# Merging the sign of float64 weights with one two-input VectorE instruction, and moving GpSimd's remainder behind the next item's addition

## The chip, the cores and the metric

The program runs on one core of a Trainium2 chip. Its engines are TensorE (PE, with its weight loads as PEld), VectorE (DVE), ScalarE (ACT), GpSimd (POOL) and SyncE (SP, which here only issues DMAs). Each engine works through its own instructions in order and waits on semaphores for the others. The metric is the device time of one execution in microseconds: the kernel before took a median of 1064.12 us in 3 runs (1062.75 to 1064.14).

## The reference, cut to what matters

Three parts follow one another: attention over 4 batches and 8 heads of 768 tokens with a mask of 8 global and 96 local positions; a routed layer of 8 experts in which each expert takes 384 of the 3072 tokens; and a dense layer with a leaky activation. The two weights of the dense layer come in double precision, and the device itself turns them into the form that it computes with.

```python
def _attn_ref(q, k, v, n_global, n_local):
    scores = scale * np.matmul(q, k.transpose(0, 1, 3, 2)) + bias      # masked
    a = np.exp(scores - np.max(scores, axis=-1, keepdims=True))
    a = a / (np.sum(a, axis=-1, keepdims=True) + 1e-09)
    return np.matmul(a, v)
...
def _moe_ref(x, w_gate, w1, w2):
    ...
    for e in range(E):
        mask = assigned == e
        out[mask] = np.maximum(x[mask] @ w1[e], 0.0) @ w2[e]
...
def _moe2_ref(x, w_in, w_out, alpha):        # w_in 512 x 2048, w_out 2048 x 512
    h = x @ w_in
    g = np.maximum(h, 0.0) + alpha * np.minimum(h, 0.0)
    return g @ w_out
```

## The kernel before

**The stages.** Attention comes first and ends near 185 us of the span; a search for the tokens of the first expert follows; from about 217 us on the experts run, one after another, each through its own layer and then through the dense one, and TensorE is nearly full there to the end. The change touches only what is woven into attention.

**Attention** (L91 to L329) works through 48 steps: 24 groups of 128 queries, each in two halves of four heads (`steps`, L284). In step n the code issues the scores of step n + 1 (L186: TensorE, then L192 on VectorE, which adds the bias and takes the minimum, then L195 on ScalarE, the exponential), the transposes of step n (L207, copied out of PSUM by L211 on VectorE and L209 on ScalarE), `divisor` (L234, a tiny GpSimd instruction named `a_se`), the combination of step n - 2 (L238, L252, L261, L271 and, in the odd steps, L274), and the values of step n - 1 (L226, L229). A batch's first group has scores 128 wide, the others 232.

**The conversion of doubles** (class `Doubles`, L31 to L88) is a generator that attention pulls twice in a step, before the scores and at the step's end, in four of every five steps (`turn`, L280). The fifth is called a free step below. It has 32 items of 128 x 512 doubles, taken by turns from `w_in` and `w_out`: an **in item** (the 1st, 3rd, ...) ends as a pair of tensors, a rounded `hi` and the remainder `lo`, both in `wi`; an **out item** (the 2nd, 4th, ...) ends in `wo` after one addition. The raw doubles lie in `f_raw` (`f64_raw` in the code), as two 32-bit words each, so one word's elements are 8 bytes apart; `f_t` (`f64_t`) takes the result. Both have three buffers.

An item takes one step. On the first pull (`begin`, L69) ScalarE makes the absolute value of the high words (L72), GpSimd clamps it (L73), ScalarE scales the low words (L74). On the second (`join`, L76) VectorE shifts and masks `f_t` (L79) and writes the sign bit into `f_raw`'s low word (L80, on 16-bit elements), and GpSimd adds the two (L82). `finish` (L84) belongs to the item before: on the first pull, behind the new item's L73, GpSimd rounds to `hi` (L87) and subtracts for `lo` (L88), for in items only. Two more raw loads are ahead on SP's queue (L67), each waiting until the addition that last read its buffer is done.

**The order** is that in which the code issues, engine by engine: nothing is rearranged afterwards. VectorE's L79 and L80 stand at the end of a step, and the four L192 for the next scores stand behind them.

Of the kernel before, what the change touches and what calls it, by code (L numbers as in the profile page):

```python
# [9 lines left out]
FT = mybir.dt.float32  # L10
# [4 lines left out]
U16 = mybir.dt.uint16  # L15
AF = mybir.ActivationFunctionType
OP = mybir.AluOpType
# [13 lines left out]
class Doubles:  # L31
# [7 lines left out]
    def jobs(self, items):  # L39
        queue, begun = [], None  # L40

        def fetch():
            if items:
                src, dst, hi, lo = items.pop(0)
                queue.append(dict(src=src, dst=dst, hi=hi, lo=lo))
                self.load(queue[-1])

        fetch()
        fetch()
        yield  # L50
        yield
        while True:
            done, begun = begun, queue.pop(0) if queue else None
            fetch()
            if begun:
                self.begin(begun)
            if done:
                self.finish(done)
            yield
            if begun:  # L60
                self.join(begun)
            self.idle = not (queue or begun)
            yield

# [10 lines left out]

    def join(self, job):  # L76
        nc, t = self.nc, job["t"]
        parts = job["raw"].bitcast(U16).rearrange("p a (b c) -> p a b c", c=2)
        nc.vector.tensor_scalar(t, t, 3, 0x7FFFFFF8, op0=OP.logical_shift_left, op1=OP.bitwise_and)  # L79
        nc.vector.tensor_scalar(parts[:, :, 0, 1], parts[:, :, 1, 1], 0x8000, None, op0=OP.bitwise_and)  # L80
        dst = t if job["dst"] is None else job["dst"].bitcast(I32)
        nc.gpsimd.tensor_tensor(dst, t, job["raw"][:, :, 0], op=OP.add)  # L82

    def finish(self, job):  # L84
        if job["hi"] is not None:
            v = job["t"].bitcast(FT)
            self.nc.gpsimd.tensor_scalar(job["hi"], v, 1.0, 1.0, op0=OP.mult, op1=OP.mult)  # L87
            self.nc.gpsimd.tensor_tensor(job["lo"], v, job["hi"], op=OP.subtract)  # L88


def attention(ctx, tc, q, k0, k, v, vw, w_gate, n_global, n_local, ident, x_dram, logits, side, router):  # L91
# [1148 lines left out]
```

## Time and profile before

| | |
|---|---|
| median of 3 runs | 1064.12 us |
| profiled execution | 1064.48 us, of which the span from the first to the last instruction is 1062.8 us |
| busy over the span | PE 97%, DVE 68%, ACT 36%, POOL 51% |
| L80, 32 instructions | 750 ns median, 1835 ns longest |
| L79, 32 instructions | 419 ns median, 1355 ns longest |
| L82, 32 instructions | 1280 to 1307 ns |
| L88, 16 instructions | 1270 to 1502 ns |

The busy shares are means over stages with different limits. The stretch that matters here is the one in which the 32 items run, from about 26 to 172 us. In a view in order of time a row gives the start, the duration, the engine, the line and the tiles; instructions of one engine that don't wait for each other overlap a little in the records, so the price of one is read from start to start.

### The profile page before, as it was taken

How to read it: one execution, taken by the hardware profiler on the slowest of the kernel's cores; microseconds unless marked ns; L12 is line 12 of the kernel's file. 1: busy time of each engine (PE TensorE's matmuls, PEld its weight loads, DVE VectorE, ACT ScalarE, POOL GpSimd, SP SyncE). 2: the span in 40 equal slices, each digit the busy share in tenths (PEclk: the TensorE clock that was granted, in tenths of full speed). 3: DMA queues.
4: the chain of work that ended last, by engine and by line, in shares of the span. 5: the costliest groups of instructions: out<-in, count | busy, mean ns of one | idle time of the engine just before them, and what ended most of it. 6: DMA issues, size and time to landing. Idle time of an engine off the chain costs nothing.

```text
span 1062.8 us, 19360 instructions
## 1 busy us (share of the span) xinstructions
PE 1027.4 (97%) x6475; PEld 904.7 (85%) x6475; DVE 725.7 (68%) x2189; ACT 386.4 (36%) x984; POOL 544.0 (51%) x825
## 2 busy tenths in 40 slices
PE   7999999699999999999999999999999999999997
PEld 5777767389889988898899889988998999999996
DVE  6999998787878778877887688689854313231321
ACT  6989988143224212321232123212321232123211
POOL 4777764175669325733473347344642464247223
PEclk9999999699999999999999999999999999999999
DMA  9899893241355244326432633443353345434131
GB/s 299 275 298 308 293 306 125 51 148 60 132 196 166 86 168 157 105 104 194 143 115 85 220 118 118 148 155 116 121 172 123 122 138 170 133 106 169 63 136 69
DMA packets 89046, 164.98 MB, mean 155 GB/s; under 512 B 9812, under 2 KB 43092, under 8 KB 88948
## 3 DMA queue, kind: packets, MB, share of 16 engines
q1 hardware_dynamic: 85108, 151.18, 42.7%
q0 software_dynamic: 3840, 12.59, 3.5%
q8 instruction: 51, 0.84, 0.3%
q14 instruction: 47, 0.39, 0.1%
HBM read 142.76 MB, written 20.97 MB: 154 GB/s over the span
## 4 chain that ended last, share of the span: by engine, by line
PE 79%; DVE 8%; POOL 4%; issue 3%; ACT 3%; DMA 2%; SPq 0%; POOLq 0%; ACTq 0%; DVEq 0%
PE m_h L969 23%; PE m_acc L1014 23%; PE m_acc L956 12%; PE m_h L929 12%; PE a_pt L207 2%; PE a_xp L226 2%; PE a_s L186 2%; ACT a_p L195 2%; DVE f_raw L80 1%; POOL m_so L898 1%; POOL m_g L898 1%; PE a_cb L252 1%; DVE a_sx L192 1%; PE m_h L855 1%; DMA f_raw<-in_moe_w_out_dram 1%
## 5 line engine op out<-in xcount | busy, mean ns | idle before, releaser
L898 POOL TENSOR_TENSOR m_g<-m_t,m_g 128x192 fp32r<-128x192 f32 (+1 forms) x286 | 163.8, 595 | 335.0 <-ACT m_g L978 334.9
L1014 PE MATMUL m_acc<-m_so,m_g 128*128 128x512 f32 x1143 | 294.1, 399 | 0.0
L969 PE MATMUL m_h<-m_y,wi 128*128 128x384 f32 x1536 | 290.2, 339 | 0.0
L969 PEld LDWEIGHTS m_h<-m_y,wi 128*128 128x128 f32 x1536 | 267.4, 188 | 6.6 <-DVE m_xt L871 0.2
L1014 PEld LDWEIGHTS m_acc<-m_so,m_g 128*128 128x128 f32 x1143 | 209.2, 189 | 34.5 <-POOL m_g L898 0.5
L898 POOL TENSOR_TENSOR m_s<-m_r,m_s 128x256 fp32r<-128x256 f32 x256 | 187.4, 756 | 77.7 <-ACT m_s L888 77.4
L978 ACT ACTIVATE m_g<-m_t 128x384 fp32r<-128x384 f32 (+1 forms) x143 | 70.0, 489 | 427.0 <-DVE m_t L977 251.3
L976 DVE TENSOR_SCALAR m_t<-m_h,m_al 128x384 f32<-128x384 f32 (+1 forms) x144 | 82.3, 571 | 155.4 <-PE m_h L969 145.1
L956 PE MATMUL m_acc<-m_hh,m_s 128*128 128x384 f32 x768 | 148.1, 339 | 0.0
L929 PE MATMUL m_h<-m_xt,m_s 128*128 128x384 f32 x768 | 144.4, 336 | 0.6 <-DVE m_xt L871 0.4
L929 PEld LDWEIGHTS m_h<-m_xt,m_s 128*128 128x128 f32 x768 | 134.5, 188 | 2.4 <-DVE m_xt L871 0.6
L956 PEld LDWEIGHTS m_acc<-m_hh,m_s 128*128 128x128 f32 x768 | 132.7, 189 | 0.0
L888 ACT ACTIVATE m_s<-m_r 128x512 fp32r<-128x512 f32 x128 | 79.7, 626 | 68.6 <-PE m_acc L956 66.9
L195 ACT ACTIVATE a_p<-a_sx,a_mn 128x232 f32<-128x232 f32 (+1 forms) x192 | 88.4, 466 | 19.5 <-DVE a_mn L192 19.3
L933 DVE SCALAR_TENSOR_TENSOR m_hh<-m_h,m_hh 128x384 fp32r<-128x384 f32 x64 | 35.5, 555 | 78.5 <-ACT m_hh L932 78.3
L977 DVE SCALAR_TENSOR_TENSOR m_t<-m_h,m_t 128x384 f32<-128x384 f32 (+1 forms) x144 | 73.9, 513 | 4.9
L781 DVE TENSOR_REDUCE r_red<-r_cmp 128x24 bf16<-128x576 bf16 (+1 forms) x97 | 73.9, 761 | 3.3
L192 DVE CUSTOM_DVE_ANT_0 a_sx<-a_s,a_bias 128x232 f32<-128x232 f32 (+1 forms) x192 | 62.4, 381 | 7.2 <-PE a_s L186 7.0
L932 ACT ACTIVATE m_hh<-m_h 128x384 fp32r<-128x384 f32 x64 | 31.5, 492 | 91.2 <-PE m_h L929 88.9
L207 PE MATMUL a_pt<-ident,a_p 128*128 128x128 f32 (+1 forms) x352 | 57.8, 289 | 6.9 <-DVE a_r L238 3.2
L207 PEld LDWEIGHTS a_pt<-ident,a_p 128*128 128x128 f32 (+1 forms) x352 | 37.6, 137 | 28.8 <-ACT a_p L195 15.2
L186 PE MATMUL a_s<-a_k,a_q 64*128 64x232 f32 (+1 forms) x384 | 50.4, 383 | 5.5 <-DMA a_q<-in_q_dram 5.5
(192 smaller groups left out, 1166.1 us busy)
## 6 DMA issues: line engine op xcount, KB each, us to landing
m_so<-wo_pairs SPq DMA_DIRECT2D x112, 512.0 KB, 3.5
m_r<-in_moe_w_dram SPq DMA_DIRECT2D x128, 256.0 KB, 3.0
a_k<-in_k_dram SPq DMA_DIRECT2D x20, 464.0 KB, 5.8
f_raw<-in_moe_w_in_dram SPq DMA_DIRECT2D x16, 512.0 KB, 6.5
f_raw<-in_moe_w_out_dram SPq DMA_DIRECT2D x16, 512.0 KB, 7.8
wo_pairs<-m_so SPq DMA_DIRECT2D x16, 512.0 KB, 2.6
a_v<-in_v_dram SPq DMA_DIRECT2D x24, 256.0 KB, 6.2
x_rows<-a_xo SPq DMA_DIRECT2D x24, 256.0 KB, 5.1
```

What stands on the lines that cost most here:

```text
L192: nc.vector.tensor_tensor_reduce(out=sx[:, s, :n], in0=ps[s][:, a, :n], in1=bs[:, h], scale=-scale, scalar=BIG, op0=OP.add, op1=OP.min, ac ...
L195: nc.scalar.activation(pr[:, s, KW - n:], sx[:, s, :n], AF.Exp, bias=T["mn", g][:, h:h + 1], scale=-1.0, accum_out=T["sum", g][:, h:h + 1])
L207: nc.tensor.transpose(ps[:, i], pr[:, :GW] if part else pr[:, GW:], ident)
L781: nc.vector.tensor_reduce(red, cmp, axis=AX.X, op=OP.add)
L888: self.nc.scalar.activation(s[:, 0], r, AF.Copy)
L898: self.nc.gpsimd.tensor_tensor(lo[:, c:c + n], x[:, c:c + n], hi[:, c:c + n], op=OP.subtract)
L929: nc.tensor.matmul(ps[:, :n], s1[:, a, d], x[:, b, d], start=(d == 0 and i == 0), stop=(d == self.ND - 1 and i == 2))
L956: nc.tensor.matmul(ps[:, :n], s2[:, b, d * 128:(d + 1) * 128], h[:, a], start=(f == 0 and a + b == 0), stop=(last and a == 1))
L969: nc.tensor.matmul(ps[:, :n], self.wi[:, a, d, f * 128:(f + 1) * 128], y[:, b, d], start=(d == 0 and i == 0), stop=(d == self.ND - 1 and i ...
L976: nc.vector.tensor_scalar(t[:, cs], ps[:, cs], 0.0, self.al[:, f:f + 1], op0=OP.min, op1=OP.mult)
L977: nc.vector.scalar_tensor_tensor(t[:, cs], ps[:, cs], 0.0, t[:, cs], op0=OP.max, op1=OP.add)
L1014: self.nc.tensor.matmul(self.ex[e]["op"][t], g[:, a, t * 128:(t + 1) * 128], s[:, b], start=(f == 0 and a + b == 0), stop=(f == self.F2 // ...
```

## The change

Three edits, all in `Doubles`. The sign is merged by one VectorE instruction with two inputs, the raw high words and `f_t`, that writes `f_t`; it stands where L80 stood. `finish` is split: `upper` (the rounding to `hi`) stays on the first pull, `lower` (the subtraction for `lo`) moves to the second pull, behind the new item's addition. The second of the two first raw loads is issued one pull later.

```diff
         fetch()
+        yield
         fetch()
-        yield
         yield
         while True:
             done, begun = begun, queue.pop(0) if queue else None
             fetch()
             if begun:
                 self.begin(begun)
-            if done:
-                self.finish(done)
+            if done and done["hi"] is not None:
+                self.upper(done)
             yield
             if begun:
                 self.join(begun)
+            if done and done["hi"] is not None:
+                self.lower(done)
...
     def join(self, job):
-        parts = job["raw"].bitcast(U16).rearrange("p a (b c) -> p a b c", c=2)
         nc.vector.tensor_scalar(t, t, 3, 0x7FFFFFF8, op0=OP.logical_shift_left, op1=OP.bitwise_and)
-        nc.vector.tensor_scalar(parts[:, :, 0, 1], parts[:, :, 1, 1], 0x8000, None, op0=OP.bitwise_and)
+        nc.vector.scalar_tensor_tensor(t, job["raw"][:, :, 1], -0x80000000, t, op0=OP.bitwise_and, op1=OP.bitwise_or)
...
-    def finish(self, job):
-        if job["hi"] is not None:
-            v = job["t"].bitcast(FT)
-            self.nc.gpsimd.tensor_scalar(job["hi"], v, 1.0, 1.0, op0=OP.mult, op1=OP.mult)
-            self.nc.gpsimd.tensor_tensor(job["lo"], v, job["hi"], op=OP.subtract)
+    def upper(self, job):
+        self.nc.gpsimd.tensor_scalar(job["hi"], job["t"].bitcast(FT), 1.0, 1.0, op0=OP.mult, op1=OP.mult)
+
+    def lower(self, job):
+        self.nc.gpsimd.tensor_tensor(job["lo"], job["t"].bitcast(FT), job["hi"], op=OP.subtract)
```

GpSimd's order before, from the second item on; `f64_t_336` is the first item (an in item), `f64_t_469` the second (an out item), `f64_t_534` the third:

```order
L73 TENSOR_SCALAR f64_t_469<-f64_t_469 128x512
L87 TENSOR_SCALAR wi_68<-f64_t_336 128x512
L88 TENSOR_TENSOR wi_68<-f64_t_336,wi_68 128x512
L234 TENSOR_SCALAR a_se_507<-a_sum_342 128x4
L82 TENSOR_TENSOR wo_69<-f64_t_469,f64_raw_276 128x512
L73 TENSOR_SCALAR f64_t_534<-f64_t_534 128x512
```

The same place in the changed kernel, where the clamp is L75, the rounding L86, the addition L83 and the subtraction L89:

```order
L75 TENSOR_SCALAR f64_t_469<-f64_t_469 128x512
L86 TENSOR_SCALAR wi_68<-f64_t_336 128x512
L235 TENSOR_SCALAR a_se_506<-a_sum_342 128x4
L83 TENSOR_TENSOR wo_69<-f64_t_469,f64_raw_324 128x512
L89 TENSOR_TENSOR wi_68<-f64_t_336,wi_68 128x512
L75 TENSOR_SCALAR f64_t_534<-f64_t_534 128x512
```

The subtraction of an in item has moved from in front of the out item's addition to behind it, and so stands in front of the next in item's clamp.

VectorE's order before at the end of a step, with the third item's two instructions:

```order
L238 RECIPROCAL a_r_575<-a_se_427 128x4
L261 TENSOR_TENSOR a_lp_574<-a_cb_570,a_r_575 128x32
L271 TENSOR_TENSOR a_xo_573<-a_cb_570,a_r_575 128x256
L79 TENSOR_SCALAR f64_t_534<-f64_t_534 128x512
L80 TENSOR_SCALAR f64_raw_334<-f64_raw_334 128x512
L192 ISA a_sx_617,a_mn_612<-a_s0_609,a_bias_100 128x232
```

And in the changed kernel, where the shift is L80 and the merge L81:

```order
L239 RECIPROCAL a_r_575<-a_se_427 128x4
L262 TENSOR_TENSOR a_lp_574<-a_cb_570,a_r_575 128x32
L272 TENSOR_TENSOR a_xo_573<-a_cb_570,a_r_575 128x256
L80 TENSOR_SCALAR f64_t_534<-f64_t_534 128x512
L81 SCALAR_TENSOR_TENSOR f64_t_534<-f64_raw_334,f64_t_534 128x512
L193 ISA a_sx_616,a_mn_611<-a_s0_608,a_bias_100 128x232
```

The instruction count is the same. The merge reads what the shift just wrote, and no longer touches the low words.

SP's queue around the first two raw loads, in the changed kernel:

```order
L132 DMA a_v<-in_v_dram 128x512
L135 DMA a_vw<-in_vw_dram 104x512
L69 DMA f_raw<-in_moe_w_in_dram 128x1024
L69 DMA f_raw<-in_moe_w_out_dram 128x1024
L126 DMA a_k<-in_k_dram 128x928
```

Between the two pulls of that step SP is given nothing else, so the two loads stand next to each other there, at the same place of the queue as before.

## Rows read from the trace of the kernel before

**Rows 1.** Busy time of each engine while the items run.
```profile
26.00:172.00 146.00, 138.84 (x1332) 107.38 (x1331) 140.66 (x565) 134.32 (x446) 108.05 (x133) 1.00 0.87 288
```

**Rows 2.** VectorE's waits, 26 to 172 us: total, times, longest.
```profile
DVE a_sx L192 <- PE a_s L186: 1.2, 1, 1.2
DVE f_t L79 <- POOL f_t L73: 0.7, 1, 0.7
...
DVE a_sx L192 <- ACT a_pts L209: 0.2, 1, 0.2
```

**Rows 3.** VectorE's groups between 20 and 180 us: busy us, mean ns.
```profile
L80 DVE TENSOR_SCALAR f_raw<-f_raw 128x512 uint16<-128x512 uint16 x32 | 34.0, 1064 | 0.0
...
L79 DVE TENSOR_SCALAR f_t<-f_t 128x512 int32<-128x512 int32 x32 | 16.5, 517 | 0.8 <-POOL f_t L73 0.7
```

**Rows 4.** VectorE in order of time: start, duration; items 18 to 21.
```profile
103.86 0.75 DVE L80 TENSOR_SCALAR f_raw<-f_raw 128x512 uint16<-128x512 uint16 x1
...
107.02 0.42 DVE L79 TENSOR_SCALAR f_t<-f_t 128x512 int32<-128x512 int32 x1
107.35 0.74 DVE L80 TENSOR_SCALAR f_raw<-f_raw 128x512 uint16<-128x512 uint16 x1
107.88 0.43 DVE L192 CUSTOM_DVE_ANT_0 a_sx<-a_s,a_bias 128x232 f32<-128x232 f32 x1
...
111.02 1.82 DVE L80 TENSOR_SCALAR f_raw<-f_raw 128x512 uint16<-128x512 uint16 x1
...
115.25 0.42 DVE L79 TENSOR_SCALAR f_t<-f_t 128x512 int32<-128x512 int32 x1
```

**Rows 5.** GpSimd in order of time, over the same items.
```profile
102.28 1.27 POOL L88 TENSOR_TENSOR wi<-f_t,wi 128x512 fp32r<-128x512 f32 x1
103.63 1.02 POOL L234 TENSOR_SCALAR a_se<-a_sum 128x4 f32<-128x4 f32 x1
...
108.18 1.30 POOL L82 TENSOR_TENSOR f_t<-f_t,f_raw 128x512 int32<-128x512 int32 x1 [1.16 <-DVE f_raw L80]
109.44 0.62 POOL L73 TENSOR_SCALAR f_t<-f_t 128x512 f32<-128x512 f32 x1
110.14 0.62 POOL L87 TENSOR_SCALAR wi<-f_t 128x512 fp32r<-128x512 f32 x1
110.84 1.40 POOL L88 TENSOR_TENSOR wi<-f_t,wi 128x512 fp32r<-128x512 f32 x1
...
112.96 1.30 POOL L82 TENSOR_TENSOR wo<-f_t,f_raw 128x512 int32<-128x512 int32 x1
114.35 0.61 POOL L73 TENSOR_SCALAR f_t<-f_t 128x512 f32<-128x512 f32 x1
```

**Rows 6.** VectorE, the first expert and a later one: a two-input instruction free.
```profile
203.46 0.36 DVE L639 TENSOR_TENSOR r_sel<-r_full,r_oh 128x192 f32<-128x192 f32 x1
...
667.65 0.62 DVE L639 TENSOR_TENSOR r_sel<-r_full,r_oh 128x192 f32<-128x192 f32 x1
```

**Rows 7.** VectorE: a copy and a product of the attention steps, 20 to 180 us.
```profile
L211 DVE COPY a_pts<-a_pt 128x512 f32<-128x512 f32 x43 | 29.5, 686 | 0.0
L271 DVE TENSOR_TENSOR a_xo<-a_cb,a_r 128x256 f32<-128x256 f32 x43 | 17.9, 415 | 0.2 <-issue 0.2
```

**Rows 8.** VectorE: an instruction that reads what the one before it wrote.
```profile
700.16 0.62 DVE L976 TENSOR_SCALAR m_t<-m_h,m_al 128x384 f32<-128x384 f32 x1 [0.43 <-PE m_h L969]
700.81 0.56 DVE L977 SCALAR_TENSOR_TENSOR m_t<-m_h,m_t 128x384 f32<-128x384 f32 x1
```

**Rows 9.** VectorE in order of time: the shortest and the longest way to an in item.
```profile
140.91 1.81 DVE L80 TENSOR_SCALAR f_raw<-f_raw 128x512 uint16<-128x512 uint16 x1
...
144.87 0.43 DVE L79 TENSOR_SCALAR f_t<-f_t 128x512 int32<-128x512 int32 x1
...
160.73 0.75 DVE L80 TENSOR_SCALAR f_raw<-f_raw 128x512 uint16<-128x512 uint16 x1
...
164.08 0.41 DVE L79 TENSOR_SCALAR f_t<-f_t 128x512 int32<-128x512 int32 x1
```

## The prediction

> **What bounds the kernel now.** I read the busy shares first. Over the whole span TensorE is fullest, but the change lies in the stretch in which the 32 items run, so the view to read is the table by stretches there: of 146 us VectorE is busy 140.7, TensorE 138.8, ScalarE 134.3, GpSimd 108.1 [rows 1]. Three engines look full, so the waits decide. VectorE waits for anything only four times in the whole stretch, 2.3 us in sum: 1.2 and 0.7 us, and two of 0.2 [rows 2]. It is the bound, it works in order, and whatever is added to it or taken from it there moves the end one to one. What comes behind (the routing, the experts) starts from attention's last step and is not touched.
>
> Then I looked for time inside VectorE's busy rows that is not work. L80 takes 1064 ns on the mean and L79 517 [rows 3], while an undisturbed pair takes 0.74 and 0.42 [rows 4]. The long ones stand beside GpSimd's subtraction L88: one starts at 110.84 and runs 1.40 us, to 112.24 [rows 5], and the L80 that starts at 111.02 ends at 112.84 [rows 4], 0.6 us behind the subtraction's end. It was held until GpSimd let go. The other way round too: the tiny `a_se` that starts at 103.63 takes 1.02 us [rows 5] and ends when the L80 of 103.86 does [rows 4]. So L79, L80 and GpSimd's instructions exclude each other.
>
> **The change part by part, per item and in sum.**
>
> *The block that goes.* With the subtraction behind the addition, no L88 runs while VectorE shifts and merges, since the addition itself waits for the merge. That gives back 34.0 - 32 x 0.75 = 10.0 us of L80 and 16.5 - 32 x 0.42 = 3.1 us of L79 [rows 3, 4]: 13.1 us. What is late next is the rounding to `hi`, which stays in front. Counted from the end of an in item's merge, the addition starts 0.09 us later (0.09 from an L80's end to L82) and the clamp 1.26 after that, the rounding 0.70 later with 0.62 of its own [rows 4, 5]: it ends at 2.67. VectorE comes to the next shift at 2.5 to 2.7 (below), so it is held for a tenth of a microsecond at the most, somewhat more in the one short step. I take 0.5 us in all.
>
> *The merge.* Before, the pair costs 0.33 + 0.53 = 0.86 us from start to start (107.02, 107.35, 107.88) [rows 4]. The merge now reads what the shift wrote. L977 reads what L976 wrote and starts 0.03 us after its end [rows 8], where L80 starts 0.09 before the end of L79. So the shift costs 0.42 + 0.03 = 0.45. For the merge itself, a two-input instruction with both inputs in SBUF takes 0.36 us at 192 columns [rows 6]; 256 columns more cost 686 - 415 = 271 ns between two groups of this stage, 1.06 ns each [rows 7]; at 512 columns that is 0.36 + 0.34 = 0.70, and 0.61 up to the start of the next. Together 1.06, so +0.20 us per item and 32 x 0.20 = +6.4 us. Nothing hides it, as VectorE is the bound.
> Bounds: the merge reads every second word. From below, it costs no more than the L80 that it replaces and its wait nothing: 0 instead of +6.4. Less than that is excluded, since 192 columns with two inputs already take 0.36 us where the shift does 512 in 0.42. From above, the same L639 took 0.62 us at 667.65, where its first input is read with a wide step [rows 6]: (0.62 - 0.36) / 192 = 1.35 ns more per column, 0.69 us per merge, 32 x 0.69 = +22 us on top. I take +6.4, because the nearest row is L80 itself: it reads and writes with this very step of 8 bytes, and 512 columns cost 0.53 us, 1.04 ns each.
>
> The Trainium skill has a rule for the step (SBUF — State Buffer, "Door 1: The DMA port swizzle"): accesses run at full rate as long as at least two fall into one line of 16 bytes. By that rule an 8-byte step is free and the sum stays; L80's 1.04 ns per column agrees. On the wait, VectorE: DVE Perf Modes, "The DRAIN you can't avoid", says that a semaphore behind each instruction costs nothing extra. By that rule the merge would start where L80 did, 0.12 us earlier, and the sum would be 32 x 0.12 = 3.8 us lower; the 0.03 us behind L976 against 0.09 us of overlap speak against it.
>
> *The wait that comes.* The subtraction, moved behind the out item's addition, now stands in front of the next in item's clamp, and that item's shift on VectorE waits for the clamp. Behind the shift in VectorE's queue stand the merge and the four L192 of the next scores, for which ScalarE and TensorE wait. From the end of an out item's merge to the end of that clamp: 0.09 to the addition, 1.39 from it to the next instruction (112.96 to 114.35), 1.35 for the subtraction (102.28 to 103.63), 0.61 for the clamp [rows 5]: 3.44 us. VectorE's own way from the end of an out item's L80 to the next in item's L79 is 2.41 us (112.84 to 115.25, and 104.61 to 107.02) [rows 4]; over the items the shortest is 2.15 and the longest 2.60 [rows 9]. Behind the merge it is 0.13 longer, as its record overlaps the next by 0.09 where L80's overlaps by 0.22. There are 15 such places, all without a free step between; one is held up by a late load anyway. The other 14: seven near 2.41 wait 3.44 - 2.54 = 0.90, four near 2.60 wait 0.71, three near 2.15 (scores of a batch's first group) wait 1.16, in sum 6.3 + 2.8 + 3.5 = +12.6 us. Before, the same chain without the subtraction ended at 2.1, in front of VectorE. The bounds are small: the chain is made of rows from start to start, and a tenth more or less is 1.4 us.
>
> *The raw loads.* SP's queue holds the two loads at the same place as before, so this edit costs and gives nothing. The other loads wait for the additions, which keep their place behind the merge. An in item's raw words may even land up to 2 us later than now, since its clamp is held longer than that.
>
> Sum: -13.1 + 0.5 + 6.4 + 12.6 = +6.4 us. On the profiled execution's 1064.48 us that is 1070.9; the median of the runs lies 0.36 lower, so 1070.5 us. The change takes a block away and puts a wait of about the same size in its place; the price of the merge decides.
>
> **The rivals.**
> *Merge and wait for free* (lower bound above): block and new wait cancel, 1064.48 + 6.4 - 6.4 - 0.36 = 1064.1 us, no change; with the wait alone for free, 1066.7. For it: L80 already does 512 columns in 0.53 us. Against it: [rows 6, 8].
> *Dear merge*: the step of 8 bytes costs what the wide step costs L639, 1070.5 + 22 = about 1092 us, or 1081 with half of it. For it: one row of a two-input read with a step. Against it: L80.
> *Faster, a short chain on GpSimd*: if addition, subtraction and clamp overlap when nothing stands between them, so that the clamp ends before VectorE needs it, the 12.6 us vanish and the time is 1057.9 us. It decides where the chain falls below 2.54 us, 0.9 less than the rows add up to. For it: GpSimd's spans are rough, and a clamp once followed an addition after 1.26 instead of 1.39 us. Against it: the spacings are from start to start, and the subtraction never stands below 1.27 us. A gain by engines that run ahead while VectorE waits is excluded: VectorE has 2.3 us of waits to get back [rows 2].
> *The change does nothing* holds for the raw loads alone.
>
> **How the numbers follow.** Forecast 1070.5 us with chance 0.60 (its own range 1067 to 1074: the wait's tenth, the block behind the rounding); free merge 0.16, nearly all of it within 0.2% (2.1 us, about what a measurement can tell from no change); dear merge 0.10; short chain 0.14. Faster 0.14, same 0.14, slower 0.72. The range runs from 1061 to 1081: below it lies most of the short chain, above it the worse half of the dear merge, and what it leaves out is below 2 in 10.
>
> **What would show it.** Right: no L80 or L81 of the new kernel above 0.8 us while GpSimd subtracts; shifts of in items that wait for the clamp, some 0.7 to 1.2 us each and 14 times; the merge near 0.70 us and 0.03 behind the shift; the additions of out items followed at once by the subtraction. Wrong: merges of 1 us or more (dear), clamps that end before VectorE comes (short chain), or waits of VectorE elsewhere that shrink by more than 2 us.

## The result, and the profile after

The changed kernel takes 1069.62 us (median of 6 runs, 1067.80 to 1071.98), the kernel before 1063.70 in the same runs: a ratio of 1.0056 with a 95% interval of 1.0042 to 1.0069, or 5.9 us slower. The forecast was 6.4 us. The profiled execution is the fastest of the six (1067.8 us, span 1066.1), so its own difference, 3.3 us of span, is smaller; a second profile below shows where that comes from. All times are medians of runs at the usual granted clock; one run of the experiment with the subtraction behind the clamp (1249.74 us at a mean granted clock of 0.751) is left out of its median.

Busy time while the items run, and VectorE's waits there:

```profile
26.00:172.00 146.00, 134.03 (x1287) 102.98 (x1281) 128.46 (x544) 130.74 (x433) 98.41 (x128) 1.00 0.84 282
```
```profile
DVE f_t L80 <- POOL f_t L75: 12.1, 15, 1.3
DVE a_lp L262 <- PE a_cb L253: 0.2, 1, 0.2
DVE a_xo L272 <- issue: 0.2, 1, 0.2
```

VectorE was busy for 140.7 us of this stretch and is now busy for 128.5 [rows 1]. Read alone, that looks like relief. The waits tell where it went: 2.3 us in four waits [rows 2] have become 12.1 us in 15 waits of the shift for GpSimd's clamp. The time in which VectorE stood still inside an instruction is now time in which it stands still in front of one. The groups of the two instructions (busy us, mean ns, idle before):

```profile
L81 DVE SCALAR_TENSOR_TENSOR f_t<-f_raw,f_t 128x512 int32<-128x512 int32 x32 | 22.4, 701 | 1.1
...
L80 DVE TENSOR_SCALAR f_t<-f_t 128x512 int32<-128x512 int32 x32 | 13.9, 435 | 12.1 <-POOL f_t L75 12.1
```

The sign instruction's mean has fallen from 1064 to 701 ns, the shift's from 517 to 435 [rows 3]. Items 18 to 21 in order of time, VectorE first:

```profile
105.45 0.41 DVE L80 TENSOR_SCALAR f_t<-f_t 128x512 int32<-128x512 int32 x1
105.89 0.69 DVE L81 SCALAR_TENSOR_TENSOR f_t<-f_raw,f_t 128x512 int32<-128x512 int32 x1
106.50 0.39 DVE L193 CUSTOM_DVE_ANT_0 a_sx<-a_s,a_bias 128x232 f32<-128x232 f32 x1
...
109.98 0.43 DVE L80 TENSOR_SCALAR f_t<-f_t 128x512 int32<-128x512 int32 x1 [0.80 <-POOL f_t L75]
110.44 0.69 DVE L81 SCALAR_TENSOR_TENSOR f_t<-f_raw,f_t 128x512 int32<-128x512 int32 x1
...
113.82 0.42 DVE L80 TENSOR_SCALAR f_t<-f_t 128x512 int32<-128x512 int32 x1
114.27 0.69 DVE L81 SCALAR_TENSOR_TENSOR f_t<-f_raw,f_t 128x512 int32<-128x512 int32 x1
...
118.36 0.43 DVE L80 TENSOR_SCALAR f_t<-f_t 128x512 int32<-128x512 int32 x1 [0.81 <-POOL f_t L75]
118.82 0.69 DVE L81 SCALAR_TENSOR_TENSOR f_t<-f_raw,f_t 128x512 int32<-128x512 int32 x1
```

GpSimd over the same items:

```profile
111.27 1.29 POOL L83 TENSOR_TENSOR f_t<-f_t,f_raw 128x512 int32<-128x512 int32 x1 [0.79 <-ACT f_raw L76]
112.53 0.61 POOL L75 TENSOR_SCALAR f_t<-f_t 128x512 f32<-128x512 f32 x1
113.22 0.62 POOL L86 TENSOR_SCALAR wi<-f_t 128x512 fp32r<-128x512 f32 x1
...
115.10 1.29 POOL L83 TENSOR_TENSOR wo<-f_t,f_raw 128x512 int32<-128x512 int32 x1 [0.79 <-ACT f_t L74]
116.36 1.26 POOL L89 TENSOR_TENSOR wi<-f_t,wi 128x512 fp32r<-128x512 f32 x1
117.71 0.61 POOL L75 TENSOR_SCALAR f_t<-f_t 128x512 f32<-128x512 f32 x1
```

Follow the 20th item, an out item: its merge starts at 114.27 and ends at 114.96; addition, subtraction and clamp follow one another with at most 0.1 us between them; the clamp ends at 118.32 and the 21st item's shift starts at 118.36, after 0.81 us of idleness. From one merge's end to the next (114.96 to 119.51) it takes 4.55 us, where the kernel before needed 3.49, from 112.84 to the end of this L80:

```profile
115.58 0.75 DVE L80 TENSOR_SCALAR f_raw<-f_raw 128x512 uint16<-128x512 uint16 x1
```

The way from an in item to the out item behind it, 111.13 to 114.96, takes 3.83 us instead of 4.75 [rows 4]. Gain and loss stand next to each other in 13 of the 15 pairs; the L80 of the 8th and the 18th item was not held by a subtraction before, and they get nothing back. Call the way from the end of one item's sign instruction to the end of the next one's a leg. From the second item to the last, the 15 legs to an in item grow from 53.2 to 68.4 us in sum, and the 15 to an out item shrink from 87.0 to 76.3. That is +15.2 and -10.7, together +4.5 us. (In GpSimd's rows the wait of an addition is put down to ScalarE; L74 and L76 had ended before, and the addition starts 0.14 us behind the merge's end, for which it waits too.)

### The profile page after: what moved, and what is told of

It is laid out like the page before. It is cut to its first block, busy times and chain, and to the rows that moved or that the text cites. A ratio compares the mean times of both kernels' runs of the same rounds, so it can differ in the third digit from the quotient of the medians.

```text
span 1066.1 us, 19358 instructions
## 1 busy us (share of the span) xinstructions
PE 1026.5 (96%) x6473; PEld 903.9 (85%) x6475; DVE 718.2 (67%) x2189; ACT 386.4 (36%) x984; POOL 538.5 (51%) x825
## 4 chain that ended last, share of the span: by engine, by line
PE 74%; DVE 5%; POOL 3%; issue 2%; DMA 1%; ACT 0%; POOLq 0%; DVEq 0%; ACTq 0%
PE m_h L970 23%; PE m_acc L1015 23%; PE m_acc L957 12%; PE m_h L930 12%; POOL m_so L899 1%; POOL m_g L899 1%; PE m_h L856 1%; PE a_pt L208 1%; PE a_xp L227 1%; DVE r_red L782 1%; PE a_s L187 1%; DVE r_over L578 1%; DMA wo_pairs<-m_so 1%; PE r_ps L715 0%; DVE r_cmp L774 0%
## 5 line engine op out<-in xcount | busy, mean ns | idle before, releaser
L957 PEld LDWEIGHTS m_acc<-m_hh,m_s 128*128 128x128 f32 x768 | 132.7, 189 | 0.0
L193 DVE CUSTOM_DVE_ANT_0 a_sx<-a_s,a_bias 128x232 f32<-128x232 f32 (+1 forms) x192 | 61.4, 375 | 5.5 <-PE a_s L187 5.0
```

The source lines that it names most:

```text
L957: nc.tensor.matmul(ps[:, :n], s2[:, b, d * 128:(d + 1) * 128], h[:, a], start=(f == 0 and a + b == 0), stop=(last and a == 1))
```

## The experiments

**The merge alone.** The edit is the one line in `join`; the subtraction stays where it was.

```diff
-        nc.vector.tensor_scalar(parts[:, :, 0, 1], parts[:, :, 1, 1], 0x8000, None, op0=OP.bitwise_and)
+        nc.vector.scalar_tensor_tensor(t, job["raw"][:, :, 1], -0x80000000, t, op0=OP.bitwise_and, op1=OP.bitwise_or)
```

> The merge alone: the subtraction for the remainder stays in front of the out item's addition. Theory (the merge costs about 0.2 us more than what it replaces, because it must wait for the shift's end, and the block by GpSimd's subtraction has nothing to do with the kind of sign instruction): merges of free items take 0.69 us and start 0.03 us behind the shift; in the out items the shift or the merge is still held until the subtraction ends; time about 1063.7 + 32 x 0.18 = 1069.4 us. Rival (the merge is free, all of the loss comes from the moved subtraction): about 1063.7 us. Second rival (two inputs are not held by GpSimd as the 16-bit form was): no merge above 0.8 us, and some 5 us less than before, 1059 us.

Measured: 1068.11 us against 1064.19, ratio 1.0039 (1.0023 to 1.0054). The rivals fall, the size is 3.9 us, under the expected 5.2 to 5.7. A blocked merge, VectorE and then GpSimd:

```profile
112.01 0.42 DVE L78 TENSOR_SCALAR f_t<-f_t 128x512 int32<-128x512 int32 x1
112.46 1.64 DVE L79 SCALAR_TENSOR_TENSOR f_t<-f_raw,f_t 128x512 int32<-128x512 int32 x1
```
```profile
112.14 1.42 POOL L87 TENSOR_TENSOR wi<-f_t,wi 128x512 fp32r<-128x512 f32 x1
```

The two-input form is held by the subtraction as the 16-bit form was: it ends at 114.10, 0.54 us after GpSimd's 113.56. And this is why the merge costs less here than 32 times its price: where it is held anyway, its later start lies inside the block. The legs show it. The 8 to an out item that hold no free step take 36.7 us in sum, 36.6 before; the 15 to an in item, where no subtraction holds the merge, take 55.7 instead of 53.2, 0.17 us more each.

**The moved subtraction alone**, with the old sign instruction: `finish` split as in the change (`lower` stands behind `join(begun)`), `join` as before.

```diff
+            if done and done["hi"] is not None:
+                self.lower(done)
```

> The moved subtraction alone, with the old 16-bit sign instruction. Theory (the move takes 13.1 us of blocks away and adds waits for the clamp of 3.44 us less VectorE's own way, 2.15 to 2.60 us): 15 waits of the shift for the clamp, 13 to 15 us in sum, no sign instruction above 1 us, time about 1063.7 - 13.1 + 1 + 14.5 = 1066 us. Rival (the merge is free and the move costs everything): about 1069.6 us. Rival (the move gains, and only the merge loses): below 1060 us.

Measured: 1065.22 us against 1064.19, ratio 1.0011 (1.0002 to 1.0021). VectorE's two groups and its wait for the clamp:

```profile
L82 DVE TENSOR_SCALAR f_raw<-f_raw 128x512 uint16<-128x512 uint16 x32 | 24.4, 762 | 0.0
...
L81 DVE TENSOR_SCALAR f_t<-f_t 128x512 int32<-128x512 int32 x32 | 14.2, 442 | 12.8 <-POOL f_t L75 12.8
```
```profile
DVE f_t L81 <- POOL f_t L75: 12.8, 15, 1.3
```

The busy time of the pair falls from 50.5 to 38.6 us (34.0 + 16.5 before [rows 3], 24.4 + 14.2 here), 11.9 less, and 12.8 us of waits come. The move is nearly an exchange at par, as the theory has it: 1.0 us slower, where the expected 1066 us meant 2.4. Two of the signs looked for were missed by a little: the waits were to sum to 13 us or more, and one sign instruction, the 8th item's beside the rounding to `hi`, takes 1.17 us. From the second item to the last, the merge alone lengthens the legs by 3.7 us and the move alone by 1.0, and the change by 4.5: the merge is the larger part of the loss.

**The raw loads alone.**

```diff
         fetch()
+        yield
         fetch()
-        yield
         yield
```

> Only the second raw load issued one pull later. Theory: SP's queue holds the same DMAs in the same order with the same waits, so 1063.7 us, within the spread of the runs. Rival (the later load takes pressure off the first loads of keys and queries): 1 us or more faster, with a shorter first wait of TensorE for its queries.

Measured: 1064.10 us against 1064.19, ratio 1.0001 (0.9990 to 1.0012). SP's queue is the same, and so is the time. The rival's 1 us lies at the interval's edge, but its sign is missing: TensorE's longest wait for its queries is 3.8 us in both traces.

**The subtractions in the free step.** Old sign instruction, `hi` of the first in item as before, and both subtractions (with the second in item's rounding) issued where no item runs:

```diff
+    def drain(self):
+        while self.late:
+            self.lower(self.late.pop(0))
+        job = self.last
+        if job and job["hi"] is not None:
+            self.upper(job)
+            self.lower(job)
+            job["hi"] = None
...
             if turn(n):
                 next(side)
+            else:
+                drain()
```

> The kernel before with its old sign instruction, and the subtractions of two in items moved into the free step, in which no item runs and VectorE has neither a shift nor a sign instruction. Theory (the subtraction costs nothing where it stands neither beside a shift nor in front of a clamp that is waited for): the 13.1 us of blocks vanish and no wait comes in their place; then ScalarE and TensorE, at 3.5 to 3.6 us a step, hold the pace, so 1052 to 1057 us. Rival (GpSimd is full: the free step cannot take 3.4 us of rounding and subtractions, and the next out item's clamp is late by 1 us): 1058 to 1062 us. Rival (attention was bound by TensorE or ScalarE all along): within 2 us of before.

Measured: 1056.52 us against 1064.19, ratio 0.9926 (0.9914 to 0.9939): 7.7 us faster than before and the fastest of all versions run. GpSimd in and behind a free step, from the second in item's addition on:

```profile
111.14 1.30 POOL L85 TENSOR_TENSOR f_t<-f_t,f_raw 128x512 int32<-128x512 int32 x1 [1.15 <-DVE f_raw L83]
112.39 1.28 POOL L91 TENSOR_TENSOR wi<-f_t,wi 128x512 fp32r<-128x512 f32 x1
113.76 0.62 POOL L88 TENSOR_SCALAR wi<-f_t 128x512 fp32r<-128x512 f32 x1
114.47 1.32 POOL L91 TENSOR_TENSOR wi<-f_t,wi 128x512 fp32r<-128x512 f32 x1
115.87 0.22 POOL L246 TENSOR_SCALAR a_se<-a_sum 128x4 f32<-128x4 f32 x1
116.17 0.61 POOL L76 TENSOR_SCALAR f_t<-f_t 128x512 f32<-128x512 f32 x1
```

Then VectorE's groups, and the stretch of the items:

```profile
L83 DVE TENSOR_SCALAR f_raw<-f_raw 128x512 uint16<-128x512 uint16 x32 | 24.3, 760 | 0.0
...
L82 DVE TENSOR_SCALAR f_t<-f_t 128x512 int32<-128x512 int32 x32 | 13.6, 425 | 1.0 <-POOL f_t L76 1.0
```
```profile
26.00:162.00 136.00, 132.71 (x1298) 104.66 (x1296) 128.53 (x554) 131.90 (x437) 102.02 (x131) 1.00 0.93 308
```

The pair's busy time is 37.9 us, near that of the move (38.6), and the wait for the clamp is down to 1.0 us. Blocks of 12.6 us are gone, and 7.7 us reach the end. The legs tell where the rest is lost: the seven that hold a free step take 50.8 us in sum, as long as before (50.4), where the move alone brings them to 45.3. Two things fill them. VectorE waits 3.4 us there, 2.2 of it for TensorE and ScalarE and 1.0 for the clamp, where the move alone left 0.2: over the whole stretch TensorE is now busy for 132.7 of 136 us and ScalarE for 131.9, both more than VectorE's 128.5. That is what the theory expected. What it left out is that the free step is not empty on VectorE. The code puts the first small instructions of the routing there, and GpSimd's work holds them as it held the shift. One of them, and GpSimd beside it:

```profile
78.19 1.13 DVE L523 TENSOR_TENSOR r_unit<-r_half 24x3 bf16<-24x3 bf16 x1
```
```profile
78.03 1.28 POOL L91 TENSOR_TENSOR wi<-f_t,wi 128x512 fp32r<-128x512 f32 x1
```

With the move alone the same instruction takes 0.15 us. Over the seven legs the routing's instructions take 4.0 us instead of 2.2.

**The same with the merge.** The edit is the first experiment's line.

> As the free-step kernel, but with the two-input merge for the sign. There VectorE waited 6 us on others and no block or wait for a clamp is left, so the merge's price is seen nearly by itself. Theory (0.17 to 0.20 us of VectorE's own time per merge, and VectorE is still within a per cent or two of being the bound): 1056.5 us plus 2 to 6 us, 1058.5 to 1062.5. Rival (the merge only cost something because it drew out the chain over GpSimd): 1056.5 us, no change.

Measured: 1058.41 us, 1.9 us more than without the merge (ratio to before 0.9945, 0.9932 to 0.9958); each of the two was measured beside the kernel before, not beside the other. This is 0.1 us below the theory's range, though the merge runs 0.692 us as ever:

```profile
L82 DVE SCALAR_TENSOR_TENSOR f_t<-f_raw,f_t 128x512 int32<-128x512 int32 x32 | 22.1, 692 | 1.1
```

The legs settle why. The 23 without a free step grow by 3.4 us in sum, 0.15 each: where VectorE is the bound, the merge is paid. The seven with a free step shrink by 1.7 us, from 50.8 to 49.1, as VectorE's waits there fall from 3.4 to 1.2 us and the routing's instructions from 4.0 to 3.3.

**The subtraction behind the clamp.** The changed kernel, with `lower` called on the first pull after that of `upper`, behind the next item's `begin`:

```diff
+            if late:
+                self.lower(late.pop())
             if done and done["hi"] is not None:
                 self.upper(done)
+                late.append(done)
...
-            if done and done["hi"] is not None:
-                self.lower(done)
```

> The changed kernel with the subtraction one place further back: behind the next in item's clamp instead of in front of it. Theory (VectorE's shift and GpSimd's instructions exclude each other, so that the wait for the clamp turns into a block of the shift by the subtraction that now stands behind the clamp, of nearly the same length): no waits for the clamp above 0.1 us in the in items, shifts of 1.0 to 1.3 us there, and 0 to 3 us less than the changed kernel, 1066 to 1070 us. Rival (what cost was the order of semaphores, not GpSimd being busy): 12 us less, 1058 us.

Measured: 1065.55 us against 1064.14, ratio 1.0012 (1.0003 to 1.0022), about 3 us under the changed kernel and just under the expected 1066 to 1070. No wait for the clamp is left. In its place stands this, the 21st item's shift and GpSimd beside it:

```profile
118.01 1.16 DVE L81 TENSOR_SCALAR f_t<-f_t 128x512 int32<-128x512 int32 x1
```
```profile
117.04 0.62 POOL L76 TENSOR_SCALAR f_t<-f_t 128x512 f32<-128x512 f32 x1
117.62 1.28 POOL L90 TENSOR_TENSOR wi<-f_t,wi 128x512 fp32r<-128x512 f32 x1
```

The clamp ended at 117.66, in good time, and the shift ran until 119.17 because the subtraction ran until 118.90. The order of the semaphores was not the cause; GpSimd being busy at that moment was.

**The subtraction twice.** The change with a second, equal `self.lower(done)` behind the first.

> The changed kernel with each of the 16 subtractions issued twice, one behind the other. Theory (15 of them stand in the chain from an out item's merge to the next in item's shift, with no slack): 15 x 1.35 = 20 us more than the changed kernel, 1089 to 1091 us, and waits for the clamp of 30 to 33 us in sum. Rival (GpSimd has slack behind the additions, or the wait is not set by the subtraction): less than 10 us more.

Measured: 1090.82 us against 1064.14, ratio 1.0243 (1.0226 to 1.0260), some 22 us above the changed kernel.

```profile
DVE f_t L81 <- POOL f_t L76: 28.9, 15, 2.6
```

The waits for the clamp grow by 16.8 us, less than the 18 to 21 expected. But all 15 legs to an in item now last 5.9 us, 20.2 us more in sum than in the changed kernel, and that is the theory's 20: in four of them VectorE stands 3.2 us in sum in front of the next scores, and that much less in front of the shift. The rest of the 22 us lies outside of these legs. The place has no slack: each further subtraction of 1.27 us costs 1.34, on an engine that is busy for half of the span.

**The changed kernel again.**

> The changed kernel once more, for a second profile: the first profile's execution was the fastest of its six. Theory (the stretch of the items takes the same time in every execution, and what varies lies outside of it, in the first loads or in the search for the first expert): intervals between merges the same within 0.1 us, median 1069.6 us within 1 us. Rival (the waits for the clamp vary from run to run): the sum of these waits differs from 12.1 us by 2 us or more.

Measured: 1068.50 us against 1064.14, ratio 1.0044 (1.0030 to 1.0057), 1.1 us below the first median, where 1 was allowed. The waits for the clamp are the same to the tenth. The first two merges and the last of this profile, then of the first one, then the second and the last L80 of the kernel before:

```profile
20.36 0.69 DVE L81 SCALAR_TENSOR_TENSOR f_t<-f_raw,f_t 128x512 int32<-128x512 int32 x1
28.66 0.69 DVE L81 SCALAR_TENSOR_TENSOR f_t<-f_raw,f_t 128x512 int32<-128x512 int32 x1
...
173.28 0.69 DVE L81 SCALAR_TENSOR_TENSOR f_t<-f_raw,f_t 128x512 int32<-128x512 int32 x1
```
```profile
20.53 0.69 DVE L81 SCALAR_TENSOR_TENSOR f_t<-f_raw,f_t 128x512 int32<-128x512 int32 x1
27.60 0.69 DVE L81 SCALAR_TENSOR_TENSOR f_t<-f_raw,f_t 128x512 int32<-128x512 int32 x1
...
172.29 0.69 DVE L81 SCALAR_TENSOR_TENSOR f_t<-f_raw,f_t 128x512 int32<-128x512 int32 x1
```
```profile
28.87 0.76 DVE L80 TENSOR_SCALAR f_raw<-f_raw 128x512 uint16<-128x512 uint16 x1
...
168.02 1.81 DVE L80 TENSOR_SCALAR f_raw<-f_raw 128x512 uint16<-128x512 uint16 x1
```

From the second merge to the last it is 144.62 and 144.69 us; from the first to the second 8.30 and 7.07. What varies between the two profiles lies in front of the second item, where VectorE still waits for the first scores (1.6 us in this profile, 0.6 in the first). In the kernel before, the ends of the same two L80 stand 140.2 us apart, so the stretch itself has grown by about 4.5 us in both profiles. The first profile's smaller difference is explained by this too: its second merge starts 1.3 us earlier than the second L80 before, and 4.5 - 1.3 is nearly the 3.3 us of span. The second median's 4.4 us is what the stretch shows; the first median's 5.9 has 1.5 us more, and where they lie is open, as none of the longer runs was profiled.

## Why the prediction was right

- **The bound.** VectorE alone set the pace while the items ran. What was added to its chain came out at the end (the subtraction twice: 20 us expected, 20.2 measured in the legs to an in item), and what was taken off came out in part, until the next engines were reached (free step).
- **The block that goes**, forecast at -13.1 + 0.5 us: the pair's excess over its free times is now 22.4 - 32 x 0.69 = 0.3 us and 13.9 - 32 x 0.42 = 0.5. This rest stands behind the rounding, where 0.5 was forecast; the one merge above 0.8 us (the 8th item's, 0.98) is held by the rounding, not by the subtraction.
- **The wait that comes**, forecast at 14 waits and 12.6 us: 15 and 12.1 us. The chain from merge to clamp measures 3.36 us in the pair shown (114.96 to 118.32), forecast 3.44: the addition starts 0.14 us behind the merge, not 0.09, but the next instruction stands 1.26 and not 1.39 us behind it. The 15th place is the one that the forecast left out because of a late load; it had waited 0.7 us before and waits 0.6 now, so 14 waits are new, with 11.5 us.
- **The merge**, forecast at 0.70 us and +6.4 us in sum: 0.693 us and 0.03 behind the shift, and from the shift's start to the next instruction's 1.05 us, forecast 1.06. But the sum is lower: a leg without a block grew by 0.15 to 0.17 us, not 0.20. One part is in the rows: the first L193 behind the merge takes 0.39 us, the L192 behind the old instruction took 0.43 [rows 4], which the forecast did not count. So this term was set some 1.5 us too high.
- **The sum.** In the forecast's terms the 15 legs to an in item were to grow by 12.6 + 15 x 0.20 = 15.6 us (measured 15.2), and the 15 to an out item to shrink by 13.1 - 0.5 - 15 x 0.20 = 9.6 (measured 10.7). Both halves hold, and no two errors cancel. That the first median's 5.9 us came so near to 6.4 is partly luck, as the items' stretch grew by 4.5.
- **The bounds.** The dear merge is excluded: 0.693 us for 512 columns with an 8-byte step. The rule of the Trainium skill on lines of 16 bytes (SBUF — State Buffer, "Door 1: The DMA port swizzle"), by which such a step is free, agrees with this row. The Trainium skill's finding that a semaphore behind each of eight copies costs nothing extra (VectorE: DVE Perf Modes, "The DRAIN you can't avoid") does not carry over to this pair: the merge starts 0.44 us after the shift, where L80 started 0.33 after it. The short chain on GpSimd did not come; addition, subtraction and clamp never overlapped by more than the 0.05 us at which records touch.
- **The raw loads** cost nothing, alone as well.

The one number that stays uncertain is the size of the whole: 4.4 and 5.9 us in two sets of runs, with the intervals overlapping from 4.5 to 6.1 us.

## What to carry to other kernels

Where VectorE and GpSimd cannot run side by side, an instruction that is moved away from a collision has to be followed to the end of its new queue: count from the instruction that releases it to the next one for which the bound engine waits, and compare that with the bound engine's own way. Here that comparison was 3.4 against 2.5 us, in rows of the old trace. The place that costs nothing is one in which the bound engine has no instruction that the moved one would hold, for as long as it runs. The free step came nearest; it still cost where the routing's small instructions stood in it. And a fall in busy time of the bound engine is no gain until its waits are read beside it.

## What the runs showed of the hardware

A two-input VectorE instruction on int32 data, both inputs in SBUF and one read at every second word, takes 0.693 us for 128 x 512, the same as the copy from PSUM of that size (0.685). GpSimd's subtraction holds it as it held the 16-bit one-input form and the 32-bit shift: a held shift ended 0.27 us after GpSimd's instruction (0.42 free), a held merge 0.54 us after it (0.69 free), so about 0.15 us of the instruction's own time had already passed while it waited. An instruction of 24 x 3 elements was held for a whole microsecond in the same way. Not every VectorE instruction is held: L192 and L211, which read the scores and transposes from PSUM, took their usual 0.39 and 0.68 us beside the addition that ran from 112.96 in the kernel before.

The merge, which reads what the shift wrote, starts 0.03 us after the shift's end, where L80 started 0.09 before it. It is not alone in this. In the trace before, L502 is independent of L271 in front of it and starts 0.09 us before its end; L503 reads what L502 wrote and starts 0.03 after:

```profile
62.41 0.42 DVE L271 TENSOR_TENSOR a_xo<-a_cb,a_r 128x256 f32<-128x256 f32 x1
62.74 0.15 DVE L502 TENSOR_SCALAR r_rows<-r_rows 24x4 int32<-24x4 int32 x1
62.92 0.16 DVE L503 TENSOR_SCALAR r_mask<-r_rows 24x4 bf16<-24x4 int32 x1
```

So of the 0.19 us that the merge adds between the starts of its neighbours, 0.12 are the wait for the shift's result, and the rest is the instruction itself.
